# Top-32 attention and two expert layers on one core: two scratch buffers for pairs of weights, two input buffers in place of three

## The chip, the cores and the metric

The kernel runs on one core of a Trainium2 chip. What is measured is the time of one execution on the device, in microseconds (us). The engines are PE (matrix products, with PEld for its weight loads), DVE (vector), ACT (scalar activations and copies), POOL and SP; SP issues most transfers. Each engine runs its instructions in the order in which they stand in its queue; an instruction that must wait holds all that stand behind it.

## The reference

Attention that keeps the 32 largest scores of each row, then two dense layers in sequence:

```python
scores = scale * np.matmul(q, k.transpose(0, 1, 3, 2))      # B=2, H=8, S=576, D=64
kth = np.partition(scores, -top_k, axis=-1)[..., -top_k:-top_k + 1]
scores = np.where(scores >= kth, scores, -1000000000.0)
attn = np.exp(scores - np.max(scores, axis=-1, keepdims=True))
attn = attn / (np.sum(attn, axis=-1, keepdims=True) + 1e-09)
x = np.matmul(attn, v)                                       # -> 1152 tokens x 512
h = x @ w_in                                                 # 512 -> 2048
x = (np.maximum(h, 0.0) + alpha * np.minimum(h, 0.0)) @ w_out
return ((x @ w_a) * (x @ w_b)) @ w_out2                      # 512 -> 1536 -> 512
```

## The kernel before, in words

**Attention.** It is cut into 72 tiles of up to 128 rows of scores. For each, four pairs of matmuls write the scores into a bank of PSUM (`ps`, L439), ACT copies them out (`s`, L442), and DVE selects: four rounds of eight maxima (L450, L459) with the found ones replaced between them (L457). ACT computes the exponentials (`ep`, L463) into the same bank, tag "S", of which there is one; so the score matmuls of a tile must wait until DVE has multiplied mask and exponentials of the tile before (L466). DVE takes the reciprocal of the sum (L471), POOL multiplies (L473). For the first batch PE transposes the result (`t`, L500 and L502; copies L501 and L503 on ACT); for the second ACT and POOL split it into halves of 16 bits (L479 to L481) and SP issues a transfer that transposes it (L495). Then `av` multiplies with v (`o`, L534 or L529) and writes the inputs of the next layer, `xT`: the high half on ACT (L542), the rest on DVE (L543).

**Layers.** The tokens form six groups, 0 to 5. The first layer (moe1: `h`, L614; `y`, L626) and the second (moe2: `ha`, `hb`, L614 or L618; `o`, L626 or L629) run in the order (1,0) (2,0) (1,1) (2,1) (1,2) (2,2) (1,3) (2,3) (1,4) (1,5) (2,4) (2,5), where (k,g) is layer k of group g. Group 0 has an input tile of its own; groups 1 to 5 take one tile each of tag "xT" (`xT_2092`, `xT_2844`, `xT_3972`, `xT_6317`, `xT_7662`). A group's first layer reads that tile; at its end `finish` writes the layer's result over it (L694 to L700, with transposes `tp`, L699), and the second layer reads that.

**Weights.** They arrive as 64-bit integers and are converted to 32-bit floats early. The first stages multiply in 32 bits; later ones in 16, with each weight split into a high and a low half. `pair` makes this split, two blocks of 128 x 512 at a time, as soon as no 32-bit stage needs them any longer: 8 pairs each of wi and wo, 6 each of wa and wb, 6 of w2. Scaling into the scratch tile `wsc` and the high half are ACT's, the low half POOL's:

```python
def pair(name, i, common):                                     # L247
    t = late[0].tile([P, 2, DM], F32, tag="tmp", name="wsc", bufs=TB)
    ...
            nc.scalar.activation(t[:, j], w, AF.Copy, scale=sc)              # L253, w2
            nc.scalar.activation(v[:, 0:DM], t[:, j], AF.Copy)               # L254
            nc.gpsimd.tensor_sub(v[:, DM:2 * DM], t[:, j], v[:, 0:DM])       # L255
    ...
                nc.scalar.activation(t[:, j], w[:, j], AF.Copy, scale=...)   # L262, wo
            nc.scalar.activation(t, w, AF.Copy, scale=sc)                    # L264, wi, wa, wb
        nc.scalar.activation(v[:, :, 0:DM], t, AF.Copy)                      # L265
        nc.gpsimd.tensor_sub(v[:, :, DM:2 * DM], t, v[:, :, 0:DM])           # L266
```

wi, wo, wa and wb are split where they lie. The blocks of w2 do not stay on the chip: SP loads each from `w_st` in memory (L251) into one of three buffers `w2s`, and stores the halves from another to `w_pr` (L256); the second layers load from there (L736) into the same three buffers.

**Order.** The program is written by three interleaved tracks with clocks of their own (attention with conversion, the layers, the background pairs); each next step is that of the track whose clock is lowest. A scheduler then places the instructions of each engine by simulated readiness, so a constant such as a count of buffers moves instructions that do not touch those buffers.

Of the kernel before, what the change touches and what calls it, by code (L numbers as in the profile page):

```python
# [38 lines left out]
W2L = 1  # L39
KB = 8  # L40
VB = 2
TB = 1
OB = 2
EB = 3
WKB = 1
PB = 3
JB = 1
XB = 3
GB = 4
LAG = 3  # L50
M1 = [[('T', 0, 0)], [('T', 0, 1)], [('T', 0, 2), ('T', 0, 3)], [('L', 0, 0), ('L', 1, 0), ('T', 1, 0)], [('T', 1, 1), ('T', 1, 2)], [('T', 1, 3)]]
# [34 lines left out]
def tile_topk_attention_moe(ctx: ExitStack, tc: tile.TileContext, qT, kT, vM, vL, wi, wo, al, wa, wb, w2, out):  # L86
# [157 lines left out]
    def pair(name, i, common):  # L244
        t = late[0].tile([P, 2, DM], F32, tag="tmp", name="wsc", bufs=TB)
        sc = wsc[name][:, 0:1] if common else wsc[name][:, i:i + 1]
        if name == "w2":  # L247
            for j in range(2):
                f = 2 * i + j
                w = w2_tile()  # L250
                nc.sync.dma_start(w, w2_st[f])  # L251
                v = w2_tile().bitcast(F16)
                nc.scalar.activation(t[:, j], w, AF.Copy, scale=sc)  # L253
                nc.scalar.activation(v[:, 0:DM], t[:, j], AF.Copy)  # L254
                nc.gpsimd.tensor_sub(v[:, DM:2 * DM], t[:, j], v[:, 0:DM])  # L255
                nc.sync.dma_start(w2_pr[f], v)  # L256
        else:
            w = wsb[name][:, 2 * i:2 * i + 2]
            v = w.bitcast(F16)
            if name == "wo":  # L260
                for j in range(2):
                    nc.scalar.activation(t[:, j], w[:, j], AF.Copy, scale=wo_sig[:, 2 * i + j:2 * i + j + 1])  # L262
            else:
                nc.scalar.activation(t, w, AF.Copy, scale=sc)  # L264
            nc.scalar.activation(v[:, :, 0:DM], t, AF.Copy)  # L265
            nc.gpsimd.tensor_sub(v[:, :, DM:2 * DM], t, v[:, :, 0:DM])  # L266
# [241 lines left out]
    def av(pair_):  # L508
# [7 lines left out]
        if g not in xts:  # L516
            if split_in[g] or gsize[g] > P:
                xts[g] = late[0].tile([P, 4, 256], F32, tag="xT", name=f"xT{g}", bufs=XB)
            else:
# [454 lines left out]
```

## Time and profile before

| what | us |
|---|---|
| median of three runs (721.69, 723.14, 1243.16) | 723.14 |
| profiled execution | 723.9 |
| its span, from the first instruction to the last | 722.0 |
| PE busy | 620.3 (86%) |
| DVE busy | 576.0 (80%) |
| ACT busy | 472.5 (65%) |
| POOL busy | 429.5 (59%) |

The first three are times of a whole execution, the rest busy times within the span. The granted clock of PE, a mean over a stretch, is 1.00 at 2.4 GHz and 0.50 at 1.2 GHz; over the span it is 0.942. One of the three runs took 1243.16 us; the median does not depend on it.

### The profile page before, as it was taken

To read this page: it belongs to the slowest core of one execution; us is meant where nothing else is said; L and a number is where in the kernel's file an instruction comes from. 1 tells how busy PE (TensorE), PEld (TensorE's weight loads), DVE (VectorE), ACT (ScalarE), POOL (GpSimd) and SP (SyncE) were. 2 spreads that over 40 slices of the span, in tenths; PEclk is the share of its full clock that TensorE was granted. 3 is DMA by queue.
4 is the path that set the end of the run, shared out by engine and by line. 5 is a ranking of instruction groups with operands and counts; after the bars stand their busy time and mean duration, and the time that the engine had idled before them with its cause. 6 is when DMAs were issued, how large, how long until landed. Compare 5 with 4: busy or idle time off the path is not lost.

```text
span 722.0 us, 14587 instructions
## 1 busy us (share of the span) xinstructions
PE 620.3 (86%) x4950; PEld 459.4 (64%) x4950; DVE 576.0 (80%) x1462; ACT 472.5 (65%) x967; POOL 429.5 (59%) x608
## 2 busy tenths in 40 slices
PE   2555758899989898879977999998899989899997
PEld 1334546678666676656735777765677767677775
DVE  4999899779999998799788889999899989322121
ACT  5957988797699896789778544556455545543232
POOL 5856788888456675679787655555355545321111
PEclk9998678999999998979996999999799999999999
DMA  6966998995440041222547544422355531102233
GB/s 183 336 201 197 308 310 272 311 340 154 137 117 25 15 113 37 78 75 80 151 138 202 155 106 109 108 56 58 47 104 125 102 64 34 34 2 59 63 128 103
DMA packets 98490, 94.55 MB, mean 131 GB/s; under 512 B 50416, under 2 KB 72688, under 8 KB 98416
## 3 DMA queue, kind: packets, MB, share of 16 engines
q1 hardware_dynamic: 97104, 91.26, 44.5%
q10 hardware_dynamic: 1312, 2.36, 1.1%
q8 instruction: 39, 0.64, 0.4%
q14 instruction: 35, 0.29, 0.1%
HBM read 74.33 MB, written 8.65 MB: 115 GB/s over the span
## 4 chain that ended last, share of the span: by engine, by line
PE 43%; DVE 22%; ACT 9%; DMA 8%; issue 6%; POOL 4%; SPq 1%; POOLq 0%; DVEq 0%; ACTq 0%
DVE wk L457 6%; PE h L614 6%; DVE m L459 6%; PE y L626 5%; PE hb L614 5%; PE ha L614 5%; PE o L626 5%; DVE e L466 3%; PE ps L439 3%; DMA pt<-e 3%; PE hb L618 2%; PE ha L618 2%; DMA w2s<-w_st 2%; DVE m L450 2%; PE o L534 2%
## 5 line engine op out<-in xcount | busy, mean ns | idle before, releaser
L459 DVE MAX8 m<-wk 128x8 f32<-128x576 f32 x216 | 163.0, 754 | 2.5
L605 POOL TENSOR_TENSOR gp<-gt,gp 128x256 f16<-128x256 f32 (+1 forms) x112 | 68.3, 612 | 119.0 <-ACT gp L604 108.4
L457 DVE MATCH_REPLACE8 wk<-m,wk 128x576 f32<-128x576 f32 x144 | 106.8, 742 | 0.0
L614 PE MATMUL h<-xT,wi_sb 128*128 128x256 f16 (+1 forms) x960 | 98.3, 251 | 2.1 <-DVE gp_n L663 0.7
L614 PEld LDWEIGHTS <-wi_sb 128*128 128x128 f16 x960 | 79.1, 98 | 23.7 <-issue 7.3
L604 ACT ACTIVATE gp<-gt 128x256 f16<-128x256 f32 (+1 forms) x112 | 43.3, 387 | 68.0 <-DVE gt L754 44.7
L626 PE MATMUL y<-wo_sb,gp 128*128 128x512 f16 x336 | 84.9, 385 | 3.1 <-ACT gp L604 2.0
L626 PEld LDWEIGHTS <-gp 128*128 128x128 f16 x588 | 54.8, 98 | 51.0 <-ACT gp L604 3.8
L439 PE MATMUL ps<-ks,qh 128*128 128x288 f32 x160 | 49.9, 395 | 40.5 <-DVE e L466 31.4
L473 POOL TENSOR_SCALAR e<-e,sm 128x576 f32<-128x576 f32 x72 | 55.2, 767 | 37.7 <-DVE sm L471 36.6
L450 DVE MAX8 m<-s 128x8 f32<-128x576 f32 x72 | 54.2, 753 | 26.3 <-ACT s L442 25.9
L754 DVE SCALAR_TENSOR_TENSOR gt<-hb,wb_inv,r 128x256 f32<-128x256 f32 (+1 forms) x48 | 21.4, 446 | 60.6 <-PE hb L614 60.3
L614 PE MATMUL ha<-xT,wa_sb 128*128 128x256 f16 (+1 forms) x576 | 66.3, 265 | 1.5 <-ACT xT L700 1.3
L614 PE MATMUL hb<-xT,wb_sb 128*128 128x256 f16 (+1 forms) x576 | 63.9, 260 | 0.7 <-DVE gt L754 0.7
L626 PE MATMUL o<-w2s,gp 128*128 128x512 f16 x252 | 63.8, 379 | 0.4 <-ACT gp L604 0.2
L439 PEld LDWEIGHTS ps<-ks,qh 128*128 128x128 f32 x160 | 29.7, 217 | 53.8 <-DVE e L466 28.6
L614 PEld LDWEIGHTS <-wa_sb 128*128 128x128 f16 x576 | 51.6, 100 | 15.8 <-issue 1.9
L466 DVE SCALAR_TENSOR_TENSOR e<-s,m,ep 128x576 f32<-128x576 f32 x72 | 58.1, 806 | 3.0 <-PE t L502 0.7
L442 ACT ACTIVATE s<-ps 128x576 f32<-128x576 f32 x72 | 46.6, 647 | 15.4 <-PE ps L439 14.9
L614 PEld LDWEIGHTS <-wb_sb 128*128 128x128 f16 x576 | 50.7, 98 | 7.7 <-issue 0.7
L195 ACT ACTIVATE rlo<-raw 128x512 int16<-128x512 uint32 x68 | 54.2, 797 | 2.0 <-DMA raw<-in_wi_dram 1.7
L463 ACT ACTIVATE ep<-s,nb 128x576 f32<-128x576 f32 x72 | 54.0, 750 | 1.8 <-DVE e L466 0.6
(204 smaller groups left out, 1435.1 us busy)
## 6 DMA issues: line engine op xcount, KB each, us to landing
w2s<-w_pr SPq DMA_DIRECT2D x48, 256.0 KB, 2.8
w2s<-w_st SPq DMA_DIRECT2D x36, 256.0 KB, 2.8
raw<-in_wi_dram SPq DMA_DIRECT2D x16, 512.0 KB, 6.9
raw<-in_wo_dram SPq DMA_DIRECT2D x16, 512.0 KB, 6.8
raw<-in_wa_dram SPq DMA_DIRECT2D x12, 512.0 KB, 5.4
raw<-in_wb_dram SPq DMA_DIRECT2D x12, 512.0 KB, 5.0
raw<-in_w_dram SPq DMA_DIRECT2D x12, 512.0 KB, 5.0
kr<-in_kT_dram SPq DMA_DIRECT2D x32, 144.0 KB, 2.9
```

The lines of the kernel that those rows point to most:

```text
L195: nc.scalar.activation(r.bitcast(I16).rearrange("p (n t) -> p n t", t=2)[:, :, 0], lo, AF.Copy, scale=2.0 ** -29)
L439: nc.tensor.matmul(ps[:, f, 0:HALF], q[:, h % 2, :], ks[h][:, f * HALF:(f + 1) * HALF], start=i == 0, stop=i == len(mm) - 1)
L442: nc.scalar.activation(s.rearrange("p (a n) -> p a n", a=2), ps[:, :, 0:HALF], AF.Copy)
L450: nc.vector.max(m8[:, 0:8], s)
L457: nc.vector.match_replace(out=wk, in_to_replace=m8[:, 8 * r - 8:8 * r], in_values=src, imm_value=NEG)
L459: nc.vector.max(m8[:, 8 * r:8 * r + 8], wk)
L463: nc.scalar.activation(ep, w2(s), AF.Exp, bias=nb, scale=0.125)
L466: nc.vector.scalar_tensor_tensor(w2(e), w2(s), m8[:, 31:32], ep, op0=ALU.is_ge, op1=ALU.mult, accum_out=sm[:, 0:1])
L473: nc.gpsimd.tensor_scalar(e, e, sm[:, 1:2], 1.0, op0=ALU.mult, op1=ALU.mult)
L605: nc.gpsimd.tensor_sub(l[:, 0:n], t[:, 0:n], h[:, 0:n])
L614: nc.tensor.matmul(dst[:, 0:n], w[a][:, c * P:(c + 1) * P], x[:, b, c, 0:n], start=k == 0, stop=k == 11)
L626: nc.tensor.matmul(dst, act[b][:, s], w[a], start=i == 0 and k == 0, stop=i == last and k == 2)
```

## The change

Two constants. `TB` is the number of scratch tiles `wsc` of `pair`, `XB` that of the input tiles `xT` of groups 1 to 5. One tile of either takes 4 KB of each of the 128 partitions, so the memory in use stays the same.

```diff
-TB = 1
+TB = 2
-XB = 3
+XB = 2
```

No instruction is added or removed; many move. Three places follow, each as the engine's rows before the change and then after it.

**PE, in the second layer of group 1** (`ha`, `hb` and `o0_3083` are that layer's; `t1`, `t2` transposes; `o_3646` attention times v; `ps_3715` the scores of tile 31, the thirty-second). Before, behind the transposes `t1_3637` and `t2_3638`, four matmuls each of `hb_3409` and `ha_3451` and ten of `o_3646`:

```order
L618 MATMUL hb_3452<-xT1_2092,wb_sb_86 128x128 x4
L629 MATMUL o0_3083<-w2s_3489,gp_n_3377 128x512
L629 MATMUL o0_3083<-w2s_3529,gp_n_3419 128x512
L439 MATMUL ps_3715<-ks06_311,qh033_3447 128x288
L618 MATMUL ha_3503<-xT1_2092,wa_sb_85 128x128 x4
L500 MATMUL t1_3706<-ident_67,e_3608 128x128 x4
L439 MATMUL ps_3715<-ks06_311,qh033_3447 128x288
L439 MATMUL ps_3715<-ks06_311,ql033_3448 128x288
L502 MATMUL t2_3707<-ident_67,e_3608 128x128
L618 MATMUL hb_3504<-xT1_2092,wb_sb_86 128x128 x4
L629 MATMUL o0_3083<-w2s_3576,gp_n_3462 128x512
L439 MATMUL ps_3715<-ks06_311,ql033_3448 128x288
```

After:

```order
L500 MATMUL t1_3637<-ident_67,e_3534 128x128 x4
L502 MATMUL t2_3638<-ident_67,e_3534 128x128
L439 MATMUL ps_3715<-ks06_311,qh033_3447 128x288 x2
L439 MATMUL ps_3715<-ks06_311,ql033_3448 128x288 x2
L618 MATMUL ha_3451<-xT1_2092,wa_sb_85 128x128 x4
L618 MATMUL hb_3452<-xT1_2092,wb_sb_86 128x128 x4
L534 MATMUL o_3646<-pt_3384,v022_3235 64x256
```

The four score matmuls, spread among those of the layer before, now stand together behind the transposes and ahead of `ha_3451`, `hb_3452` and `o_3646`.

**ACT, in the split of w2** (`r` and `gp` belong to the first layer of group 2, `t` are transposes, `ks` and `qh` attention's inputs). Before:

```order
L253 ACTIVATE wsc<-w2s,w_sc 128x512
L604 ACTIVATE gp<-gt 128x256
L649 ACTIVATE r_4502<-h,pre_sig 128x256
L254 ACTIVATE w2s<-wsc 128x512
L542 ACTIVATE xT_3972<-o,vsc 128x64
L604 ACTIVATE gp<-gt 128x256
L357 ACTIVATE qh_4391<-qr_4388 128x256
L442 ACTIVATE s<-ps 128x576
L253 ACTIVATE wsc<-w2s,w_sc 128x512
```

After, from the third block on:

```order
L253 ACTIVATE wsc<-w2s,w_sc 128x512
L254 ACTIVATE w2s<-wsc 128x512
L649 ACTIVATE r_4178<-h,pre_sig 128x256
L253 ACTIVATE wsc<-w2s,w_sc 128x512
L604 ACTIVATE gp<-gt 128x256
L649 ACTIVATE r_4242<-h,pre_sig 128x256
L501 ACTIVATE pt<-t_4271 128x4x128
L254 ACTIVATE w2s<-wsc 128x512
```

The scalings of successive blocks (L253) stand closer together; between two of them there is less other work.

**SP, at the same place** (`qr`, `kr` attention's inputs, `pt` its transposes). Before:

```order
L251 DMA w2s<-w_st 128x512
L495 DMA_TRANSPOSE pt<-e_4485 128x9x128
L256 DMA w_pr<-w2s 128x1024
L251 DMA w2s<-w_st 128x512
L352 DMA qr_4641<-in_qT_dram 64x2x64
L333 DMA kr_4629<-in_kT_dram 64x576
L334 DMA kr_4629<-in_kT_dram 64x576
```

After:

```order
L251 DMA w2s<-w_st 128x512
L352 DMA qr_4388<-in_qT_dram 64x2x128
L353 DMA qr_4388<-in_qT_dram 64x2x128
L256 DMA w_pr<-w2s 128x1024
L251 DMA w2s<-w_st 128x512
L256 DMA w_pr<-w2s 128x1024
L251 DMA w2s<-w_st 128x512
L256 DMA w_pr<-w2s 128x1024
```

Eleven of the twelve loads of w2 now stand ahead of the first transposing transfer (`e_4485`), where before three did.

## Rows read from the trace of the kernel before

**Rows 1.** The page: busy time of the engines, and the chain that ended last.

```profile
PE 620.3 (86%) x4950; PEld 459.4 (64%) x4950; DVE 576.0 (80%) x1462; ACT 472.5 (65%) x967; POOL 429.5 (59%) x608
...
PE 43%; DVE 22%; ACT 9%; DMA 8%; issue 6%; POOL 4%; SPq 1%; POOLq 0%; DVEq 0%; ACTq 0%
```

**Rows 2.** Windows: stretch, length; busy by engine (instructions); granted clock; DMA share, GB/s.

```profile
180.15:246.19 66.04, 59.97 (x474) 41.52 (x473) 63.18 (x184) 56.36 (x116) 38.23 (x43) 1.00 0.28 79
246.19:292.65 46.46, 42.70 (x293) 34.85 (x294) 37.56 (x102) 36.10 (x75) 30.51 (x41) 0.93 0.26 72
292.65:325.54 32.89, 25.01 (x168) 18.77 (x168) 30.36 (x71) 26.94 (x52) 23.47 (x45) 0.84 0.24 71
325.54:368.60 43.06, 41.84 (x360) 29.70 (x359) 37.53 (x90) 36.64 (x76) 37.89 (x56) 1.00 0.43 119
368.60:401.71 33.11, 23.09 (x168) 15.36 (x168) 27.90 (x74) 25.28 (x50) 27.01 (x40) 0.74 0.61 167
401.71:622.00 220.29, 211.60 (x1726) 152.57 (x1725) 200.19 (x484) 114.14 (x232) 115.78 (x187) 0.98 0.40 88
```

**Rows 3.** Timeline: start, duration (us), engine, line; PE at 566, ACT at 581.

```profile
566.87 0.39 PE L614 MATMUL hb<-xT,wb_sb 128*128 128x256 f16 x2
...
581.51 0.28 ACT L542 ACTIVATE xT<-o 128x128 f16<-128x128 f32 x1 [3.56 <-PE o L529]
```

**Rows 4.** Lines of `pair`: ns min/median/max; then who waited for L266 (us, times).

```profile
L264 ACT ACTIVATE wsc<-wi_sb,wi_sc x8: 1132/1149/1194, 185.0 to 224.7; 128x1024 f32<-128x1024 f32 x8
...
L262 ACT ACTIVATE wsc<-wo_sb,wo_sig x16: 707/721/786, 229.7 to 270.0; 128x512 f32<-128x512 f32 x16
...
L265 ACT ACTIVATE wo_sb<-wsc x8: 1040/1072/1107, 231.4 to 270.8; 128x1024 f16<-128x1024 f32 x8
L265 ACT ACTIVATE wa_sb<-wsc x6: 1043/1049/1057, 279.1 to 306.0; 128x1024 f16<-128x1024 f32 x6
...
  ACT wsc L264: 4.2, 5
  ACT wsc L262: 1.3, 2
...
L253 ACT ACTIVATE wsc<-w2s,w_sc x12: 705/722/725, 345.4 to 398.8; 128x512 f32<-128x512 f32 x12
...
L254 ACT ACTIVATE w2s<-wsc x12: 612/617/636, 346.5 to 399.5; 128x512 f16<-128x512 f32 x12
```

**Rows 5.** DVE: timeline at 279 and 292; waits in stretches two and three.

```profile
279.21 0.81 DVE L466 SCALAR_TENSOR_TENSOR e<-s,m,ep 128x576 f32<-128x576 f32 x1
...
292.65 0.76 DVE L450 MAX8 m<-s 128x8 f32<-128x576 f32 x1 [5.59 <-ACT s L442]
...
DVE m L450 <- ACT s L442: 8.4, 4, 5.6
DVE xT L543 <- ACT xT L542: 1.7, 1, 1.7
```

**Rows 6.** PE: timeline, the matmuls around the last scores of that tile.

```profile
290.71 1.02 PE L629 MATMUL o<-w2s,gp_n 128*128 128x512 f32 x2
291.17 0.70 PE L439 MATMUL ps<-ks,ql 128*128 128x288 f32 x1
```

**Rows 7.** ACT: timeline, the copy of these scores.

```profile
291.90 0.65 ACT L442 ACTIVATE s<-ps 128x576 f32<-128x576 f32 x1 [0.71 <-PE ps L439]
```

**Rows 8.** ACT: timeline of L253; loads L251, who waited and landing (us min/med/max).

```profile
351.90 0.72 ACT L253 ACTIVATE wsc<-w2s,w_sc 128x512 f32<-128x512 f32 x1
...
356.12 0.72 ACT L253 ACTIVATE wsc<-w2s,w_sc 128x512 f32<-128x512 f32 x1 [1.96 <-DMA w2s<-w_st]
...
361.13 0.72 ACT L253 ACTIVATE wsc<-w2s,w_sc 128x512 f32<-128x512 f32 x1
...
364.70 0.72 ACT L253 ACTIVATE wsc<-w2s,w_sc 128x512 f32<-128x512 f32 x1 [0.43 <-DMA w2s<-w_st]
...
  ACT wsc L253: 3.3, 3
...
DMA to landing us min/median/max: 2.6/3.1/4.0
```

**Rows 9.** DVE: waits in stretch five.

```profile
DVE m L450 <- ACT s L442: 3.2, 4, 1.7
DVE gt L650 <- ACT r L649: 1.5, 1, 1.5
DVE e L114 <- ACT yb L684: 0.3, 1, 0.3
```

**Rows 10.** PE: longest wait in stretch five.

```profile
PE tp L699 <- ACT yb L694: 3.0, 1, 3.0
```

## The prediction

> **What bounds the kernel now.** I began with the busy shares and the chain of work that ended last [rows 1]: PE 86%, DVE 80%, and of the chain 43% PE, 22% DVE. Neither is the bound throughout, so I cut the span at the starts of attention tiles and read busy time by stretch [rows 2]. Stretch one (180 to 246 us, tiles 17 to 25) holds DVE busy 63.18 of 66.04 us. From 401.71 us (tile 45 on) PE works 211.60 of 220.29 us, and past it the matmuls' tail follows. Between lie stretch two (tiles 26 to 30, 46.46 us), three (31 to 35, 32.89), four (36 to 40, 43.06) and five (41 to 44, 33.11), in which neither is full: DVE stands idle 8.9, 2.5, 5.5 and 5.2 us, PE 3.8, 7.9, 1.2 and 10.0 us. The granted clock averages 0.93, 0.84, 1.00 and 0.74 there, so part of those stretches ran at 1.2 GHz in place of 2.4. The pairs of weights are split exactly in stretches one to five; there alone the first constant can act. The instructions from tile 45 on keep their order, so a gain or loss before 402 us moves the end by as much, since PE has no slack behind it.
>
> **The change part by part.**
>
> *Inputs' buffers, three to two.* The third tile of inputs must now wait until the first has been read, and so on. The tightest of the three such places: the last read of the third input is a matmul that starts at 566.87 us, the first write of the fifth an ACT copy at 581.51 us [rows 3]. Slack: 14.6 us less the 0.39 us of the read. In the changed order, too, PE reads the old inputs before it makes the outputs that overwrite them. Cost 0; if all of the 14 us went elsewhere it would grow from there, and nothing below moves that place by more than 9 us.
>
> *Scratch, one to two.* With one scratch tile, ACT may not begin a pair until POOL has subtracted the pair before. That wait is priced in the trace: ACT sat idle 4.2 us in five places ahead of the scaling of wi, wa and wb, and 1.3 us in two ahead of wo [rows 4]; 5.5 us in all, and none of it on the engine that bounds its stretch. I do not book it as a gain. What counts is that the order of the work changes with it: the pairs come earlier and closer together. A wi, wa or wb pair costs ACT 1.15 + 1.05 = 2.2 us, a wo pair 2 x 0.72 + 1.07 = 2.5, a block of w2 0.72 + 0.62 = 1.34 [rows 4]. Counting the rows of the order between the tiles' score copies: five wo pairs move from stretch two to one; three wb pairs from four to three, and one w2 block with them; of the w2 blocks, six stood in four and six in five, and now one stands in three and eleven in four. No work is added or removed.
>
> Stretch one: ACT gains 5 x 2.5 = 12.5 us and stands at 56.36 + 12.5 = 68.9, over the stretch's 66.04. **+2.8 us**. Low bound +1.5 (DVE stays the limit: the rows of its changed order in this stretch sum, by their durations in the trace, to 1.5 us more), high bound +6 (ACT cannot be filled better than DVE is now, 63.18/66.04 = 0.957; 68.9/0.957 = 72).
>
> Stretches two and three: DVE waited 8.4 us for score copies and 1.7 us for an xT copy here [rows 5], the largest 5.59 us at 292.65. Why: the selection that frees the score bank had ended at 280.0 [rows 5], yet the last of that tile's score matmuls ran only at 291.17, between matmuls of the second layer's group [rows 6]; ACT copied the scores at 291.90 [rows 7] and DVE could begin. In the changed order all four of those score matmuls (ps_3715) stand ahead of two of these blocks and of the o matmuls. So the 5.59 us go, and the 1.7 us behind them, since that copy comes from the same o matmuls that stood between: −7.3. Against it, stretch three takes three wb pairs and a w2 block on ACT: 26.94 + 6.6 + 1.3 = 34.8 against 32.89, +1.9. **−5.4 us.** Low bound −8 (all DVE waits but the 2 us that PE's own work needs), high bound +4 (the score matmuls come forward but the next engine in line, ACT or POOL, keeps DVE as long, and the 1.9 doubles).
>
> Stretch four: this part loses. A w2 block is loaded from memory into one of three buffers, converted, and stored from another. In the two places where ACT waited for such a load, one block followed the other by 356.12 − 351.90 = 4.22 and 364.70 − 361.13 = 3.57 us, mean 3.9 [rows 8]. Spread among other work that was hidden but for 3.3 us [rows 8]. Now eleven blocks stand in the stretch, with between some of them one copy of 0.4 us only; eleven steps of 3.9 are 42.9 us, and with the ACT work ahead of the first and behind the last (about 4.6 us, from the rows of its order by their durations in the trace) 47.5. **+4.5 us** on 43.06. ACT runs in order, so behind a late load stand the score copies, the exponentials and the splits for DVE, POOL and PE. Low bound 0 (loads go out two ahead and the 44 us are as they were), high bound +9 (ACT's own 36.6 + 2.5 us, 9 us of waits and the 4 us that it idled for others).
>
> Stretch five: all six w2 blocks leave, 8.0 us less on ACT (25.28 to 17.3). DVE's waits were 3.2 us for score copies, 1.5 for the activations' copies and 0.3 for a square [rows 9], 5.0 together. PE's longest wait, 3.0 us for yb, had two w2 copies of ACT ahead of it [rows 10]. **−5.0 us**; low bound −6.7 (DVE full, and its small operations gone forward), high bound −1 (the waits belong to the end of the group, whose squares, scales and transposes follow each other whatever ACT does).
>
> Sum: +2.8 − 5.4 + 4.5 − 5.0 = **−3.1 us**. The profiled execution's own time is 723.9 (span 722.0), so 720.8; the median of the runs is 0.8 lower, 723.1, so **720.0**.
>
> Here a rule speaks for more. The Trainium skill, "Perfetto Trace Analysis", section "Optimization Strategy", says that the same gap repeating on the engine that should be saturated can mean too few buffers for the next tile. By that rule all 5.5 us of ACT's waits would come back at once, 717.6 in place of 720.0, and fewer input buffers would be suspect. The trace disagrees on the condition: the engine that waits is ACT, busy 56.36 of 66.04 us in stretch one, not the one that is full there.
>
> **The rivals.**
>
> *Faster.* The stretches two and five both give all that their bounds hold and four loses nothing: +1.5 − 8 + 0 − 6.7 = −13.2, so 710. For it: DVE has just that idle time, and PE, no longer idle, would not fall to 1.2 GHz (0.84 and 0.74 in three and five, each fall behind PE's waits). Against: all four bounds must hold at once, and the load chain has a measured step. Beside it stands the Trainium skill, "TensorE: Matmul & The Clock Gate", section "What's actually happening": the throttled state is the default and activity releases it; the trace agrees so far as the low clock stands where PE idles.
>
> *Slower.* The w2 loads queue behind each other and hold ACT. It decides where ACT's work between two blocks' scalings is under the load's 3.1 us: in the changed order that is so in seven of eleven places, by the durations of the rows between; three waits of this kind show before [rows 8]. Full price +9 in stretch four, with +6 in one, while the waits recovered in two and three come to −3 and five gives −1 as its group's end was late anyway: +11, so 734. For it: the steps of 4.22 and 3.57 us are measured. Against: as ACT stalls, nothing else fills POOL or DVE, so part must come back in five.
>
> *Nothing.* ACT and POOL are off the chain (9% and 4%), the scratch wait moves and the same DVE waits come back elsewhere: 723.
>
> **How the numbers follow.** The net of a gain and a loss of like size: 0.50 for about 720 (715 to 724), 0.17 for no change or a little above (724 to 729), 0.18 for the faster case (705 to 715), 0.15 for the slower (729 to 742). The range 709 to 733 leaves a tenth on either side. Within 2% (708.7 to 737.6, about what a measurement of this kernel can tell) lie all of the first two, 0.10 of the faster and 0.09 of the slower: 0.86; faster 0.08, slower 0.06.
>
> **What would show it.** Right: no ACT wait on POOL for the scratch; the 5.6 us gap of DVE gone; tile 45's selection at about 399 in place of 402; ACT waits for w2 loads of 7 us or more in all, most in tiles 36 to 40, and none after. Wrong: waits for those loads under 4 us (then faster), or stretch five as long as before though ACT has less to do (then slower); a wait of ACT's xT copies on PE's reads of older inputs would refute the zero for the inputs' buffers.

## The result: 0.6% slower, and the profile after

The changed kernel takes 725.8 us (median of 17 runs) where the kernel before takes 722.3 (17 runs): 1.0057 times as long, 95% interval 1.0033 to 1.0081, so 2.4 to 5.9 us slower. Forecast were 3 us of gain. The difference is small and clear, and of the other sign.

The profiled execution of the changed kernel is one of its faster ones (span 721.3 us). Its page, busy time of the engines and the chain that ended last:

```profile
PE 615.1 (85%) x4950; PEld 455.9 (63%) x4950; DVE 571.5 (79%) x1462; ACT 468.5 (65%) x967; POOL 429.7 (60%) x608
...
PE 53%; DVE 11%; ACT 10%; DMA 10%; issue 4%; POOL 4%; SPq 1%; POOLq 0%; ACTq 0%; DVEq 0%
```

Against [rows 1] the busy times are the same to within 1%; of the chain PE has more and DVE less, 53 and 11% here (46 and 17% in the second profile below), against 43 and 22%. The stretches, cut at the same tiles as [rows 2] (length; busy by engine; granted clock; DMA share, GB/s), and behind them tile 45 to 65 and 65 to the end:

```profile
177.85:249.24 71.39, 62.30 (x474) 43.60 (x472) 64.94 (x188) 65.25 (x130) 47.47 (x49) 0.95 0.26 73
249.24:289.80 40.56, 35.28 (x241) 29.12 (x243) 34.70 (x95) 25.25 (x56) 19.22 (x31) 0.92 0.21 62
289.80:325.51 35.71, 30.17 (x197) 21.71 (x194) 31.69 (x74) 32.39 (x60) 32.02 (x51) 0.90 0.27 78
325.51:375.22 49.71, 44.82 (x382) 31.58 (x380) 38.94 (x92) 38.26 (x86) 38.89 (x61) 1.00 0.64 184
375.22:404.10 28.88, 19.66 (x162) 13.66 (x163) 25.61 (x70) 18.88 (x37) 19.70 (x35) 0.82 0.46 112
404.10:551.73 147.63, 142.54 (x1184) 104.72 (x1182) 140.95 (x342) 77.29 (x158) 78.37 (x127) 0.99 0.40 87
551.73:721.32 169.59, 161.30 (x1507) 118.28 (x1504) 82.48 (x206) 69.09 (x163) 56.74 (x99) 1.00 0.28 69
```

Every sign of the forecast by stretch is there, and every size is worse than forecast: +5.4, −5.9 and +2.8, +6.7, −4.2 us, together +4.7 at tile 45 where −3.1 was expected. (Tiles are counted from one; ps_3715 of the section on the change belongs to the thirty-first.) The tail, from tile 45 to the end, gives 3 us back, and tile 17 begins 2.3 us earlier, before any pair: so this one profile ends 0.7 us below the profile of before, though the medians differ the other way. One profile of each could not decide; a second of each does, below.

Three things that the prediction named do show. ACT waits on POOL for the scratch in one place only, 1.5 us, in place of [rows 4]'s 5.5. The gap of 5.59 us at tile 31 [rows 5] is gone:

```profile
289.80 0.74 DVE L450 MAX8 m<-s 128x8 f32<-128x576 f32 x1
```

And ACT waits for the loads of w2 in ten places, 8.6 us in all, where [rows 8] has three and 3.3 (from the view of L253, the idle time before it):

```profile
  DMA w2s<-w_st: 8.6, 10
  POOL wb_sb L266: 1.5, 1
```

### The profile page after: what moved, and what is told of

Its sections match the earlier page's. It is cut to its first block, busy times and chain, and to the rows that moved or that the text cites. A ratio compares the mean times of both kernels' runs of the same rounds, so it can differ in the third digit from the quotient of the medians.

```text
span 721.3 us, 14596 instructions
## 1 busy us (share of the span) xinstructions
PE 615.1 (85%) x4950; PEld 455.9 (63%) x4950; DVE 571.5 (79%) x1462; ACT 468.5 (65%) x967; POOL 429.7 (60%) x608
## 4 chain that ended last, share of the span: by engine, by line
PE 53%; DVE 11%; ACT 10%; DMA 10%; issue 4%; POOL 4%; SPq 1%; POOLq 0%; ACTq 0%; DVEq 0%
PE ha L614 8%; PE hb L614 8%; PE o L626 7%; PE h L614 7%; PE y L626 7%; DMA w2s<-w_st 4%; PE ps L439 3%; DMA pt<-e 3%; PE o L629 2%; DVE wk L457 2%; DVE m L459 2%; PE o L529 2%; PE hb L618 2%; PE ha L618 2%; PE y L629 2%
## 5 line engine op out<-in xcount | busy, mean ns | idle before, releaser
L626 PE MATMUL y<-wo_sb,gp 128*128 128x512 f16 x336 | 83.0, 379 | 2.8 <-POOL gp L605 1.8
L614 PE MATMUL ha<-xT,wa_sb 128*128 128x256 f16 (+1 forms) x576 | 65.8, 264 | 1.1 <-ACT xT L700 1.1
L457 DVE MATCH_REPLACE8 wk<-m,s 128x576 f32<-128x576 f32 x72 | 53.4, 741 | 0.0
```

Of the source, the lines that this page charges most:

```text
L457: nc.vector.match_replace(out=wk, in_to_replace=m8[:, 8 * r - 8:8 * r], in_values=src, imm_value=NEG)
L614: nc.tensor.matmul(dst[:, 0:n], w[a][:, c * P:(c + 1) * P], x[:, b, c, 0:n], start=k == 0, stop=k == 11)
L626: nc.tensor.matmul(dst, act[b][:, s], w[a], start=i == 0 and k == 0, stop=i == last and k == 2)
```

## The experiments

All are edits of the two kernels, timed beside runs of the kernel before on the same chip. In the table "against before" is the ratio on record for the runs made side by side, with its interval; it is not the quotient of the medians. "Tile 17 to 45" is the length of stretches one to five, and the idle time of PE is each window's length less its PE busy time, from tile 17 to the end.

| kernel | median us | against before (95%) | tile 17 to 45 | 45 to end | PE idle |
|---|---|---|---|---|---|
| before | 722.3 | | 221.6 | 320.3 | 43.4 |
| inputs_two (same order as before) | 720.4 | 0.997 (0.994 to 1.001) | 221.0 | 320.4 | 45.8 |
| changed kernel | 725.8 | 1.006 (1.003 to 1.008) | 226.3 | 317.2 | 47.4 |
| after_again (the same) | 724.1 | 1.005 (1.002 to 1.009) | 228.6 | 317.7 | 47.8 |
| scratch_wi_wo | 725.4 | 1.004 (1.002 to 1.007) | 222.4 | 324.4 | 50.3 |
| scratch_wa_wb | 724.7 | 1.000 (0.996 to 1.004) | 219.8 | 324.9 | 44.1 |
| scratch_wo (one run) | 722.0 | | 220.0 | 323.3 | 45.2 |
| scores_37_first | 727.3 | 1.008 (1.006 to 1.011) | 224.9 | 324.9 | 46.6 |
| w2_held | 734.6 | 1.018 (1.013 to 1.024) | 234.9 | 323.0 | 54.5 |
| w2_no_wait (one run) | 727.4 | | 227.3 | 322.3 | 48.4 |
| w2_into_scratch | 726.6 | 1.007 (1.004 to 1.010) | 225.2 | 321.5 | 44.3 |
| w2_into_scratch_one | 728.5 | 1.008 (1.005 to 1.011) | 222.1 | 326.4 | 50.5 |
| before_scores_first | 719.5 | 0.997 (0.995 to 1.000) | 219.6 | 318.7 | 40.7 |
| after_scores_first | 725.2 | 1.005 (1.002 to 1.007) | 214.2 | 330.9 | 46.9 |
| after_scores_w2_scratch | 722.3 | 0.999 (0.996 to 1.002) | 215.6 | 329.3 | 42.1 |
| scores_first_w2_scratch | 712.0 | 0.988 (0.983 to 0.992) | 216.2 | 315.5 | 39.3 |
| scores_first_again (the same) | 711.9 | 0.985 (0.980 to 0.989) | 215.5 | 316.8 | 35.4 |

### Which of the two constants, and what repeats

inputs_two sets the input buffers alone:

```diff
-XB = 3
+XB = 2
```

> The scratch stays single, the input tiles go from three to two; every engine has the same instructions in the same order as before. Theory 'the scratch is the whole change': 722 us, within 1 us of before. Theory 'a missing input buffer holds the copies into xT': some 2 to 4 us more, with a wait of L542 on matmuls of an older group in the trace.

720.4 us, not distinguishable from before; every engine has the same instructions in the same order. The prediction's zero for the input buffers holds, and the loss comes with the scratch. (Three input buffers together with two scratch tiles were not run; in the changed kernel, too, ACT's copies into xT waited only for the matmuls whose result they copy.) Because the order is that of before, its profile is also a second one of before:

```profile
178.41:244.42 66.01, 59.95 (x473) 41.51 (x473) 63.16 (x184) 56.41 (x116) 38.23 (x43) 1.00 0.26 79
244.42:290.25 45.83, 42.07 (x293) 34.13 (x294) 37.55 (x102) 35.79 (x75) 30.49 (x41) 0.96 0.23 73
290.25:324.61 34.36, 26.06 (x177) 19.27 (x176) 30.42 (x72) 27.02 (x52) 25.25 (x47) 0.85 0.24 68
324.61:367.50 42.89, 41.49 (x351) 29.06 (x351) 37.63 (x89) 36.34 (x76) 36.50 (x54) 1.00 0.46 122
367.50:399.43 31.93, 19.27 (x162) 13.30 (x161) 27.78 (x73) 25.41 (x50) 26.18 (x39) 0.84 0.63 173
```

after_again is the changed kernel unedited.

> The changed kernel a second time, for a second profile. If the shifts by stretch of its first profile are of the order of the instructions (+5.4, -5.9, +2.8, +6.7, -4.2 us in stretches one to five), each comes back within 1 to 2 us; what lies before tile 17 (-2.3 us) and behind tile 45 (-3.1 us) does not come back if it is spread from run to run. Time 725 to 727 us.

```profile
179.08:250.65 71.57, 62.26 (x474) 43.62 (x472) 64.94 (x187) 65.26 (x130) 47.46 (x49) 0.95 0.25 73
250.65:291.00 40.35, 35.20 (x241) 29.05 (x243) 34.71 (x96) 25.36 (x56) 19.34 (x32) 0.92 0.22 62
291.00:326.67 35.67, 30.24 (x197) 21.71 (x194) 31.69 (x74) 32.34 (x60) 31.94 (x51) 0.90 0.27 78
326.67:376.92 50.25, 45.25 (x382) 31.52 (x380) 38.77 (x93) 38.26 (x86) 38.78 (x61) 1.00 0.60 181
376.92:407.65 30.73, 21.60 (x163) 14.67 (x164) 25.79 (x71) 18.79 (x37) 19.92 (x35) 0.78 0.44 107
```

Stretches one to four repeat within 0.6 us in the changed kernel and within 1.5 in the order of before, the fifth within 2: they belong to the order. Tile 17 does not: it begins at 178 to 180 us in these four. Of the tail, 317.2 and 317.7 against 320.3 and 320.4 us, the 3 us given back do repeat. In the order of before, behind tile 45 (first the kernel before, then inputs_two):

```profile
401.71:552.00 150.29, 143.88 (x1177) 105.63 (x1176) 138.73 (x335) 78.37 (x157) 78.70 (x128) 0.97 0.42 96
552.00:722.03 170.03, 162.03 (x1509) 118.24 (x1506) 83.59 (x208) 70.51 (x164) 57.10 (x99) 1.00 0.27 67
...
399.43:548.16 148.73, 143.18 (x1183) 105.51 (x1181) 138.75 (x337) 78.39 (x157) 79.09 (x129) 0.98 0.42 96
548.16:719.83 171.67, 163.60 (x1509) 119.36 (x1506) 83.72 (x208) 70.58 (x164) 57.16 (x99) 0.99 0.27 67
```

As many matmuls stand there as in the changed kernel, to within 6. PE is busy with them for 305.9 and 306.8 us, and in the changed kernel for 303.8 and 303.9: 2.5 of the 2.9 us are busy time. The granted clock goes the same way, 0.50 for some 10 us behind tile 45 in the order of before and for 3.4 us in the changed kernel. The means of two and two: stretch one +5.5, two −5.7, three +2.1, four +7.0, five −2.7, so +6.1 at tile 45; tail −2.9; together +3.2 us from tile 17 on, against 3.5 in the medians.

### Halves of the scratch

Each kernel here uses two scratch tiles for some weights, and one for the rest:

```diff
-        t = late[0].tile([P, 2, DM], F32, tag="tmp", name="wsc", bufs=TB)
+        t = late[0].tile([P, 2, DM], F32, tag=scratch(name in ("wi", "wo")), name="wsc", bufs=1)
+    def scratch(two):
+        last[0] = 1 - last[0] if two else 0
+        return f"tmp{last[0]}"
```

With `("wa", "wb")` and `("wo",)` in its place for the other two.

> Two scratch tiles for wi and wo alone, one for wa, wb and w2. The wi and wo pairs stand as early as in the changed kernel, the blocks of w2 as late as before (tiles 38 to 44). Theory 'early wo pairs fill ACT in stretch one and the w2 blocks cost in stretch four, each on its own': stretch one +5 us, two and three together -3 to -5, four and five 0; 722 to 725 us. Theory 'only the w2 blocks cost': 718 to 719 us. Theory 'it takes both': 722 us.

> Two scratch tiles for wa and wb alone, one for wi, wo and w2. wi and wo pairs stand as before, the w2 blocks as early as in the changed kernel (tiles 36 to 40). Theory 'two prices, each on its own': stretch one 0, two and three -3 to -5, four +6, five -4; 718 to 722 us. Theory 'the w2 blocks alone cost it all': 725 to 726 us, with ACT waiting over 7 us for the loads of w2.

> Two scratch tiles for wo alone: the wi pairs stand as before (tiles 17 to 23), six wo pairs in stretch one where before had three and the changed kernel eight. Theory 'wi pairs packed into tiles 18 to 20 are the price of stretch one' (there the step from tile 19 to 20 went from 5.0 to 7.8 us): stretch one 66 to 67 us. Theory 'ACT's load by the wo pairs': 7.5 us more on ACT, stretch one 68 to 69.5 us.

Windows of stretches one and four of scratch_wi_wo, of two, three and four of scratch_wa_wb, and of one of scratch_wo:

```profile
178.14:247.79 69.65, 60.79 (x473) 42.43 (x472) 65.09 (x187) 65.34 (x130) 47.51 (x49) 0.98 0.26 75
...
324.89:367.70 42.81, 40.12 (x340) 27.83 (x340) 36.96 (x89) 35.84 (x76) 37.20 (x54) 1.00 0.44 126
```

```profile
244.67:285.08 40.41, 36.64 (x251) 29.76 (x252) 37.65 (x103) 34.65 (x70) 28.69 (x39) 0.92 0.22 67
285.08:315.95 30.87, 27.14 (x188) 21.11 (x188) 29.67 (x68) 29.84 (x56) 29.19 (x45) 0.89 0.28 82
315.95:370.22 54.27, 48.79 (x404) 33.35 (x398) 39.90 (x94) 41.43 (x92) 43.76 (x68) 1.00 0.58 175
```

```profile
176.96:245.96 69.00, 60.92 (x474) 41.79 (x472) 64.90 (x187) 61.49 (x124) 42.83 (x45) 1.00 0.25 76
```

The price of stretch one comes with the wo pairs: +3.0 us with three more of them and the wi pairs as before, inside the 68 to 69.5 us of the theory of ACT's load; +3.6 with all eight. That ACT's load is how they lengthen it is not shown: ACT was busy 61.49 of 69.00 us there and 65.25 of 71.39 in the changed kernel, not full. Two waits of PE in stretch one of the changed kernel are not there before, both for DVE:

```profile
PE h L614 <- DVE xT L543: 1.3, 1, 1.3
PE y L629 <- DVE gp_n L663: 1.0, 1, 1.0
```

Both waits, 1.3 and 0.9 us, recur in scratch_wi_wo and w2_into_scratch. With wi and wo pairs at these places nine profiles have 69.4 to 72.1 us (mean 70.4), seven with the pairs as before 65.8 to 66.9. The two of the changed kernel lie high, by the step from tile 17 to 18: 13.9 and 14.0 us, where w2_into_scratch below, in the same order up to there, has 12.1. The same 77 matmuls of PE took 12.0 us of this step in the changed kernel, at a mean granted clock of 0.88, and 10.3 us in w2_into_scratch, at 1.00. So 1.8 of the 5.5 us go with the clock and not with the order alone: in both profiles of the changed kernel it stood at 0.50 for 3.4 us there, behind a wait of PE for a load of w2 (1.85 and 2.04 us; w2_into_scratch has the wait, 1.72, without the fall).

The gain of stretch two is there in all of them, 5 to 7 us. So it does not need both edits; it is counted once in the changed kernel though two moves would each have brought it. The price of stretch four comes with the early w2 blocks alone, and is larger there: 54.3 us. None of this adds up to the totals, though. Of the two halves with an interval only scratch_wi_wo is slower clear of noise, by 0.2 to 0.7%; for scratch_wa_wb the interval is −0.4 to +0.4%. In the profiles scratch_wa_wb stands 1.5 us better than before at tile 45 and scratch_wi_wo 1.1 worse, and both lose 4 us in the tail, where PE's wait for a transposing transfer between tiles 65 and 69 grows from 1.9 us to 4.5 and 5.3.

### What lengthens stretch four: the loads or the queue

The prediction held ACT's waits for the w2 loads to be the cause. Per tile, the changed kernel's loss stands in one place: the step from tile 36 to 37 takes 17.2 us in both profiles, 7.4 and 7.0 in the order of before; the other four steps of the stretch are 3 us shorter together. PE, timeline of the changed kernel:

```profile
331.99 2.76 PE L626 MATMUL y<-wo_sb,gp 128*128 128x512 f16 x12
334.40 0.61 PE L439 MATMUL ps<-ks,qh 128*128 128x288 f32 x2
334.85 0.42 PE L439 MATMUL ps<-ks,ql 128*128 128x288 f32 x2
335.11 2.79 PE L614 MATMUL h<-xT,wi_sb 128*128 128x256 f16 x24
...
338.29 1.46 PE L626 MATMUL y<-wo_sb,gp 128*128 128x512 f16 x6
339.39 0.61 PE L439 MATMUL ps<-ks,qh 128*128 128x288 f32 x2
339.84 0.42 PE L439 MATMUL ps<-ks,ql 128*128 128x288 f32 x2
```

PE waits for little in this step (1.9 us), it is busy; the tile's score matmuls (eight here, four for most tiles) stand between others, the last behind 123 other matmuls since those of tile 36, 72 of them the layers' (before: 37, of them 32; the 103 of the expectation below is not what the trace shows), with 14.7 us of PE's work in place of 6.2. DVE gets its scores at 342.68:

```profile
342.68 0.76 DVE L450 MAX8 m<-s 128x8 f32<-128x576 f32 x1 [1.75 <-ACT s L442]
```

That is the pattern of the gap at tile 31 in before [rows 5, 6], moved to another tile. Four kernels set the two causes against each other. scores_37_first raises the priority of the score matmuls of tile 37 in the changed kernel; w2_held writes the w2 blocks later; w2_no_wait scales another block; w2_into_scratch loads each block into its half of a scratch tile, past the three buffers. The edit of scores_37_first:

```diff
-                nc.tensor.matmul(ps[:, f, 0:HALF], q[:, h % 2, :], ...)
+                with tc.high_priority(offset=100 if tl is tiles[36] else 0): nc.tensor.matmul(
+                                 ps[:, f, 0:HALF], q[:, h % 2, :], ...)
```

w2_held, in the track of the pairs:

```diff
-                clock["bg"] = max([clock["bg"]] + [native_used.get((name, f), 0) for f in fs])
+                clock["bg"] = max([clock["bg"] + (50 if name == "w2" and i == 0 else 0)] + [native_used.get((name, f), 0) for f in fs])
```

w2_no_wait, in `pair`:

```diff
-                nc.scalar.activation(t[:, j], w, AF.Copy, scale=sc)
+                nc.scalar.activation(t[:, j], wsb["wi"][:, f].bitcast(F16)[:, 0:DM], AF.Copy, scale=pre_w2)
```

w2_into_scratch, in `pair`:

```diff
-                w = w2_tile()
+                w = t[:, j]
                 nc.sync.dma_start(w, w2_st[f])
```

> The changed kernel with a higher priority for the score matmuls of the 37th tile alone, so that they stand together on PE behind 62 matmuls of the layers after those of tile 36, where the changed kernel has them split, the last behind 103; the w2 blocks stay in tiles 36 to 40. In both profiles of the changed kernel the step from tile 36 to 37 took 17.2 us, before 7.2. Theory 'the place of the score matmuls in PE's queue': that step comes back to 7 to 11 us and stretch four from 50 to 43 to 46. Theory 'the chain of w2 loads holds ACT': ACT's waits for these loads stay at 8 to 9 us and stretch four at 48 to 50.

> The changed kernel with the w2 blocks written later in the program: six up to tile 38, the other six at tiles 45 to 47, where PE is full and ACT half idle. The score matmuls of tile 37 stand as in the changed kernel. Theory 'loads of w2': ACT's waits for them fall from 9 to about 4 us, stretch four to 44 to 46; 720 to 722 us. Theory 'place of the score matmuls': 17 us from tile 36 to 37 as before, stretch four at 48 to 50. Either way PE may then wait at 410 to 440 us for w2 blocks that are not yet split; then some us are lost there.

> The changed kernel with w2 scaled from a block of wi that lies on the chip, so that ACT does not wait for the loads of w2 (they are still issued); the split of w2 is left out of the result in that way. The order moves too: the score matmuls of tile 37 stand together behind 21 matmuls of the layers, those of tile 38 are split, the last behind 86. Theory 'loads of w2': ACT's waits at the scaling are 0 and stretch four is 41 to 44 us. Theory 'place of the score matmuls': the slow step moves from tile 37 to 38 and stretch four stays above 46.

> The changed kernel, but each block of w2 is loaded straight into its half of a scratch tile (of which there are two) and scaled there, so that the loads no longer pass through the three buffers w2s, which hold only the halves on their way out; up to four loads can be under way. The w2 blocks stand even closer, at tiles 36 to 38. Theory 'ACT's waits for the w2 loads set stretch four': these waits (8.6 and 9.1 us in the two profiles) fall under 2 us, stretch four comes from 50 to 43 to 45 us, stretches four and five together from 79.8 to 72 to 75; 718 to 721 us. Theory 'it is the density of ACT's and POOL's work in stretch four, not the loads': stretch four stays at 48 to 52 us; 724 to 728 us.

scores_37_first: the step fell from 17.2 to 11.0 us as the queue's theory had it, but the one from tile 39 to 40 rose from 9 to 14.6, with 12.5 us of PE's work ahead of that tile's score matmuls, and stretch four stayed at 51.4, where the queue's theory had 43 to 46. ACT's waits stayed at 8.6, so this run by itself decides nothing.

w2_held: inconclusive as a test. The second layer's own loads took one of the three buffers early, the waits rose to 16.2 us in place of falling, and the step to tile 37 took 19.1 us.

w2_no_wait: the wait went only one instruction on. ACT no longer stood still ahead of the scaling but 8.7 us ahead of the copy of the high half, whose buffer was still in use for a load or a store; stretch four was 52.4 us. The slow step did move to tile 38, as the queue's theory had it (14.1 us, 11.0 of them PE's work).

w2_into_scratch did cut the waits, though not under the 2 us forecast (view of L253), and the two stretches stayed as long as they were, 79.8 us together where the changed kernel has 78.6 and 81.0:

```profile
  DMA wsc<-w_st: 3.8, 4
...
323.73:377.41 53.68, 49.63 (x401) 34.25 (x396) 39.28 (x93) 39.71 (x90) 41.56 (x65) 0.97 0.63 194
377.41:403.55 26.14, 19.66 (x152) 13.97 (x152) 25.00 (x69) 18.23 (x36) 17.96 (x31) 0.74 0.40 89
```

Its slow step is from tile 38 to 39, 15.4 us with 13.3 of PE's work. So less than half of the waits, and no gain in length: the waits for the loads do not by themselves set these two stretches. They are not cleared of a part either, since the order moved too and a step behind 13.3 us of PE's work is new; PE's idle time in the two stretches fell, from 14.1 us in both profiles of the changed kernel to 10.6.

> The changed kernel (two scratch tiles, w2 early at tiles 36 to 43, loads through the three buffers w2s as before) with a higher priority for the score matmuls of all tiles, so that the layers' matmuls between those of one tile and the next number 11 to 73 in tiles 27 to 41, where the changed kernel has up to 103 and before up to 92. Theory 'a tile takes the longer of DVE's 6 to 8 us and PE's work that stands ahead of its score matmuls': no step of 14 us or more in tiles 26 to 43, stretches four and five together 72 to 76 us (changed kernel 78.6 and 81.0), total 712 to 718 us. Theory 'ACT's waits for the w2 loads': with 5 us or more of them left, stretch four stays at 48 us or more and the total at 722 to 726 us.

after_scores_first keeps the early w2 blocks and the three buffers and puts all score matmuls first (`if True` in the edit of scores_37_first). Waits of L253, and the windows from stretch one to the end:

```profile
  DMA w2s<-w_st: 4.0, 6
...
177.89:247.25 69.36, 60.55 (x473) 42.60 (x472) 64.93 (x187) 65.22 (x130) 47.45 (x49) 0.98 0.26 76
247.25:286.65 39.40, 34.24 (x223) 26.94 (x224) 35.52 (x98) 23.39 (x51) 17.57 (x30) 0.91 0.22 64
286.65:317.37 30.72, 28.51 (x203) 22.30 (x198) 29.80 (x69) 29.51 (x58) 27.21 (x47) 1.00 0.29 89
317.37:359.82 42.45, 40.82 (x363) 29.01 (x364) 37.71 (x92) 36.29 (x80) 40.19 (x61) 1.00 0.54 156
359.82:392.04 32.22, 19.70 (x151) 12.43 (x150) 28.34 (x70) 24.38 (x47) 24.77 (x39) 0.82 0.66 171
392.04:543.46 151.42, 141.45 (x1140) 101.52 (x1139) 141.88 (x338) 76.39 (x155) 77.40 (x126) 0.96 0.40 83
543.46:722.92 179.46, 172.86 (x1594) 126.53 (x1592) 83.96 (x208) 71.81 (x169) 57.75 (x101) 1.00 0.26 68
```

The stretches do what the queue's theory says: no step over 12 us, four and five together 74.7, two and three 70.1 in place of 76, tile 45 reached 12 to 14 us sooner after tile 17 than in the changed kernel. (The waits for loads fell too, to 4.0, so they are not excluded as a part of stretch four.) But the total was forecast at 712 to 718 and is 725.2. All of the lead is gone by the end, since PE has done 44 fewer of the layers' matmuls by tile 45 and does them behind: 141.45 + 172.86 = 314.3 us of PE work are left there, 303.8 in the changed kernel. Reaching a tile earlier was no gain at all.

### What decides the end, and a faster version

That run shows a better account. In all 17 profiles of these kernels PE's busy time from tile 17 to the end lies between 492 and 503 us (mean 498.8, standard deviation 3.0), and most of its spread goes with the time that PE spent at the low clock (correlation 0.87). The time from tile 17 to the end goes from 531.6 to 557.9, and PE's idle time, 35.4 to 54.5, goes with it (correlation 0.89). The two add up to that time by definition, so both have to be looked at: w2_into_scratch and scratch_wa_wb have the idle time of before (44.3 and 44.1 us; 44.6 is the mean in the order of before) and end 5 and 3 us later, by 502.4 and 500.7 us of busy time in place of 497.1. PE's idle time by stretch, in us:

| PE idle in | one | two | three | four | five | 45 to 65 | 65 to end | sum |
|---|---|---|---|---|---|---|---|---|
| before | 6.1 | 3.8 | 7.9 | 1.2 | 10.0 | 6.4 | 8.0 | 43.4 |
| inputs_two | 6.1 | 3.8 | 8.3 | 1.4 | 12.7 | 5.6 | 8.1 | 45.8 |
| changed kernel | 9.1 | 5.3 | 5.5 | 4.9 | 9.2 | 5.1 | 8.3 | 47.4 |
| after_again | 9.3 | 5.2 | 5.4 | 5.0 | 9.1 | 5.7 | 8.1 | 47.8 |
| after_scores_first | 8.8 | 5.2 | 2.2 | 1.6 | 12.5 | 10.0 | 6.6 | 46.9 |
| scores_first_again | 5.9 | 3.9 | 4.9 | 0.0 | 8.5 | 7.3 | 4.9 | 35.4 |

The change adds 3.1 us of idle PE in stretch one, 3.6 in four and 1.4 in two, and takes 2.6 from three, 2.2 from five and 0.4 from the tail: +3.0 us, the measured loss to within its interval. PE's busy time hardly differs, 497.3 against 497.1 us, but only in sum: stretch one has 2.3 us more, at a granted clock of 0.95 in place of 1.00, and the tail 2.5 less. This is an account, not yet a cause; the causes are the waits behind it. Two of stretch one are shown above. In stretch four PE's waits in the changed kernel are led by two that before does not have (view of PE's waits):

```profile
PE o L529 <- DMA pt<-e: 1.8, 1, 1.8
PE t L502 <- ACT pt L501: 1.1, 1, 1.1
```

the transposing transfers, which SP issues between the loads and stores of w2, and ACT's copies, which stand behind its w2 work. That the w2 blocks cause these waits is argued from the order, not shown: which of them would vanish with the blocks elsewhere was not measured.

before_scores_first is the priority for all score matmuls on the kernel before (one scratch tile), w2_into_scratch_one the loading into the scratch on the kernel before, scores_first_w2_scratch and scores_first_again both together, after_scores_w2_scratch both together on the changed kernel.

> One scratch tile, as before, and a higher priority for the score matmuls of all tiles: those of tile 31 stand together, without moving the pairs. Theory 'the gain in stretch two is the place of the score matmuls alone': the wait of 5.6 us at tile 31 goes, the step from tile 30 to 31 falls from 16.4 to 7 to 10 us and stretches two and three together get 3 to 6 us shorter; 717 to 720 us. Theory 'that gain needs the earlier pairs': no gain there, 722 us.

> The same loading into the scratch with one scratch tile, in the order of before with the w2 blocks at tiles 38 to 45. Theory 'waits for the w2 loads': there were 2.4 to 2.9 us of them in stretch four and 0.9 in five, so 1 to 3 us are to be had; 719 to 722 us. Theory 'density': nothing to be had, 722 us.

> One scratch tile, higher priority for all score matmuls and the w2 blocks loaded into the scratch; they stand at tiles 40 to 46. If both gains are real and add: 716 to 719 us. If the second is nothing: 719.5 us as with the priority alone.

> The fastest kernel so far a second time (one scratch tile, score matmuls first, w2 into the scratch): 710 to 714 us, 1.0 to 1.7% under before.

> The same with the w2 blocks loaded into the two scratch tiles (blocks at tiles 37 to 40). Theory of the place of the score matmuls: about the same as the run beside it, within 3 us. Theory of the w2 loads: faster than the run beside it by the waits that go, 4 us or more.

The priority alone brings 0.3% (719.5 us), with the step to tile 31 at 11.0 in place of 16.7 (7 to 10 was forecast), stretch two 5.1 us shorter and the pairs of that stretch where they were: the gain in stretch two is the place of the score matmuls. The loading alone makes it slower by 0.8%, against both theories; ACT's waits for the w2 loads rose, from 3.3 to 9.6 us, its stretches one to five are as before (222.1 us) and its tail is 6 us longer, not explained here. Together they are the fastest, 712.0 and 711.9 us in two sets of runs, 1.2 to 1.6% under before, and faster than the 716 to 719 us of two gains that add. Why the loading costs by itself and gains 7.5 us with the priority is not shown. Stretch four of scores_first_again, and the two that follow:

```profile
321.92:359.51 37.59, 37.59 (x328) 27.08 (x327) 34.99 (x86) 32.14 (x67) 34.45 (x50) 1.00 0.32 76
359.51:393.63 34.12, 25.66 (x210) 17.94 (x208) 29.61 (x77) 27.30 (x55) 28.29 (x42) 0.80 0.72 182
393.63:537.38 143.75, 136.41 (x1108) 98.12 (x1107) 136.82 (x332) 79.11 (x160) 81.27 (x129) 0.98 0.45 109
```

PE is never idle in stretch four here. With two scratch tiles the same two edits give 722.3, 3.0 us under after_scores_first with ACT's waits down from 4.0 to 1.0: between the two theories, so a part of the loads stays possible. In both pairs of kernels that differ by the scratch and little else (719.5 against 725.2, 712 against 722.3) the second scratch tile costs 5.7 and 10.3 us, more than in the kernel as it was. Its part in stretch one is the same in all, 2.8 to 3.8 us of idle PE.

## Why the prediction was wrong

**What held.** The zero for the input buffers (inputs_two). The waits for the scratch: gone but for 1.5 us, and the kernel no faster. The rule that the prediction set beside its sum, of the Trainium skill, "Perfetto Trace Analysis", section "Optimization Strategy", is on repeated gaps of the engine that should be saturated; ACT, busy 56.36 of 66.04 us in stretch one, was not that engine, and its 5.5 us did not come back. The gap at tile 31, and its reason, the place of the score matmuls. ACT's waits for the w2 loads, forecast at 7 us or more and measured at 8.6 and 9.1. And that the second scratch tile would pay in stretches one and four and earn in two and five.

**What failed first: the sizes.** At tile 45 the sum was −3.1 and is +6.1. By terms, forecast and mean of two profiles each: stretch one +2.8, measured +5.5; two and three −5.4, measured −3.6; four +4.5, measured +7.0; five −5.0, measured −2.7. Each lies within the bounds given for it, but all four on the bad side. For stretch one, the prediction put the whole price down to ACT's load; ACT was never full there (65.25 of 71.39 us), and of the 5.5 us measured 2.3 are PE's busy time at a lower granted clock, a term that the sum did not have, and 3.1 PE's idle time. For stretch four, the prediction looked for the place of the score matmuls only at tile 31, where they moved forward, and not at the other tiles. The 17.1 us of PE's work that had stood between the scores of tiles 30 and 31 went elsewhere: 10.9 us ahead of tile 28's scores, 10.4 ahead of 32's, 14.7 ahead of 37's (before: 8.4, 5.4 and 6.2). That last step cost 9.8 us and took the place of the one removed; the term was put down to the loads of w2, whose waits were there as forecast; w2_into_scratch had less than half of them and the same length, so they are not the whole price, and how much is theirs stays open. (In the high bound of this term, 2.5 us more of ACT's work is a slip: by the prediction's own counts five more w2 blocks, 6.7 us, come and three wb pairs, 6.6, go.) For stretch five, it counted all of DVE's waits as recoverable; for score copies 1.5 and 2.3 us stayed in the two profiles and for activations' copies 0.9 and 1.2, as its own high bound allowed.

**What failed second: the step "The instructions from tile 45 on keep their order, so a gain or loss before 402 us moves the end by as much, since PE has no slack behind it".** The traces show another order there: between the score matmuls of tiles 47 and 48 stand 54 of the layers' matmuls before and 68 after, between those of 50 and 51 61 and 40, and PE's order is the same again only from about 631 us on. Nor is PE's work cut off at tile 45. A kernel that reaches it early with fewer layers' matmuls done pays them behind it (after_scores_first: 12 us in the lead, and no gain). The changed kernel reached tile 45 with as many done as before, and of its 6.1 us 2.9 were given back behind it, 2.5 of them PE's busy time at a granted clock of 0.99 in place of 0.98; why the clock fell for less time there stays open. The tile starts on DVE were the wrong ruler; PE's idle time, with its busy time beside it, is the better one.

**The rivals.** "Slower", at 0.15, was the sign, by the right stretches, with a mechanism of which the runs bear out the waits but not the price, and at a third of that price. "Nothing", at 724 to 729, has the measured time in its range. The granted clock does not tell the two kernels apart over the span (0.942 and 0.943 in the first profiles, 0.943 and 0.950 in the second), but by stretch it does, as said, and in sum these parts cancel.

## What to carry to other kernels

When the order of work changes on engines that share two streams, do not add up stretches cut by one stream's progress; account the idle time of the engine whose total work is fixed and which ends last, and beside it the busy time, which here moved with the clock. Look at every place where the short, urgent work (here the scores of the next tile) stands in that engine's queue, and how much of the other stream lies between two of them: over tiles 26 to 43, of 46 steps of 10 us or more in these profiles 43 had 8 us or more of PE's work between the score matmuls, and of 243 shorter steps 32 (many are the same step in kernels of the same order). A gap that a reordering removes can be the same work moved ahead of another tile, as here, and a priority for the urgent work, tried by itself and together with what it then exposes, is a cheap test.

## What was not expected of the hardware

Most steps from tile to tile repeat between executions far better than the whole: from tile 30 to 31, 6.19 and 6.19 us in the two profiles of the changed kernel; 36 to 37, 17.17 and 17.15. Some do not: 37 to 38 took 8.64 and 9.64 us there, and 35 to 36 in the order of before 5.42 and 7.41. The spread of the totals (719 to 726 us before but for the one run named ahead, 722 to 731 after) comes from elsewhere, in part from before tile 17, which starts between 176 and 182 us in the 17 profiles, though the pairs, and with them most of the edits, begin only there. The chain of w2 loads went a little slower than estimated: eleven steps from 322.85 to 368.32 us, 4.1 each where 3.9 had been worked out. The granted clock averaged 0.73 to 0.88 in stretch five, in which PE stood idle 21 to 40% of the time, in every kernel; the Trainium skill's "TensorE: Matmul & The Clock Gate", section "What's actually happening", says that activity releases a clock that is throttled by default, and the rows agree so far as the low clock stands where PE idles.
